# The fourth output product split into quarters, in blocks 3 to 8 of a linear-attention and feed-forward kernel

## The chip, the cores and the metric

The kernel runs on one core of a Trainium2 chip. The metric is the time of the whole kernel on the device in microseconds (us), as the median of several runs. The profile comes from one further execution, which has its own time.

## The reference

There are 8 batches of 576 tokens with 8 heads of 64 features, all in float32, so 4608 rows of 512 features. Cut to what matters:

```
kv  = einsum('bhsd,bhse->bhde', k, v)
att = einsum('bhsd,bhde->bhse', q, kv)
att = att / sqrt(mean(att * att, axis=-1) + 1e-06) * g_norm
x   = att, laid out as (4608, 512)
h   = x @ w_in                 # (4608, 512) @ (512, 2048)
g   = maximum(0.01 * h, h)     # leaky relu
out = g @ w_out                # (4608, 2048) @ (2048, 512)
```

The two products with `w_in` and `w_out` are nearly all of the work.

## The kernel before

**Blocks and chunks.** The rows are worked in 9 blocks of 512 tokens, i = 0 to 8. The 2048 hidden features are worked in 4 chunks of 512, c = 0 to 3. For a block and a chunk there is a hidden product (512 features of h for 512 tokens), a leaky relu, and an output product that adds its share to the block's 512x512 output. The text calls the output product of block i and chunk c pass n, with n = 4(i - 1) + c. Block 0 is done plainly. From block 1 on there are 32 passes, n = 0 to 31.

**Strassen's method.** Both products are cut into 2x2 parts and done with 7 products of parts instead of 8, in Winograd's form. Some factors are sums of parts. For the left side these are made by GpSimd in `sums_of` (L840), from g, into the tiles gs1 to gs4. For the right side they are made once from `w_out` and kept in device memory (`w2_dram`); SP loads them again for every pass, in `sides_w2` (L663), into the tiles `t12` and `t34`. `strassen` (L797) runs the products. In the output, products 1, 6, 7 and 4 go one after the other into one PSUM bank and add up there; products 2, 5 and 3 go into another. The two banks are called oa and oc and change roles from pass to pass. Each product is four matmuls of 128 rows by 256 columns. After each one, `done` (L990) adds the bank, or copies it where chunk 0 begins a fresh output, into one of the block's four output tiles, which are named 11, 12, 21 and 22 for their place in the 2x2 output.

**A second level.** From block 2 on the hidden product is done with two levels (`product_h_two`, L931): seven steps k = 1, 2, 6, 5, 7, 3, 4, each of seven matmuls of 128x128 in two of the banks ha, hb, hc, hd. The second bank of each step has three columns of 128 in use. The fourth column takes one quarter of the output's product 2 of an earlier pass, which is also done with a second level (`Second`, L906), so a hidden step is eight matmuls of 128x128. After the step ScalarE copies, or VectorE adds, the first three or four columns to the quarter sums `qa` and `qc` (L952, L954), and then VectorE adds the fourth column to the output tile. `inner_g` (L894) makes the sums of g's quarters that `Second` needs, on GpSimd.

**The order of the work.** It is written out by hand. A loop over the blocks, the chunks and seven slots t = 0 to 6 issues in each slot first one hidden step, then attention's next piece for a later block, then one step of the output product (`go_o`). The output product runs late: product 1 of pass n comes at slot 2 of the following chunk, product 5 at slot 3, product 6 at slot 4, nothing at slot 5, product 7 at slot 6, and products 3 and 4 at slots 0 and 1 of the chunk after that. At a chunk's end VectorE assembles g from the quarter sums with seven adds (L960 to L969), ScalarE applies the relu to the four parts of g, and GpSimd starts `sums_of`. `pin` keeps each engine's instructions in the order in which they are written; each engine works through its own instructions in that order. Inside a block, chunk 3's slots 20 to 22 also form the sums of the next block's x, on VectorE.

## Time and profile before

| what | value |
|---|---|
| median of 3 runs | 918.76 us (918.22 to 924.06) |
| the profiled execution | 917.78 us, span 916.1 us |
| TensorE busy (matmuls) | 909.3 us, 99% |
| VectorE busy | 631.6 us, 69% |
| ScalarE busy | 328.2 us, 36% |
| GpSimd busy | 370.2 us, 40% |
| DMA traffic | 200.05 MB |

In the profile PE is TensorE, DVE is VectorE, ACT is ScalarE, POOL is GpSimd, and SP is the queue that issues most DMAs. A group's line has the source line, the engine, the operation, `out<-in` by tile names, the shapes, the count, the busy time, the mean of one in ns, and the idle time of the engine just before, with what ended it. A line of the timeline has the start, the duration, the engine and the instructions merged; idle time ahead of it stands in brackets. A float32 matmul appears as two records, so a product of four matmuls is `x8`. The end of a matmul in the records is modelled; the distance between starts is safer. All engines' adds are issued by one helper (L637), so a group is told by its tiles. A line of the list of waits gives who waited, for whom, the total in us, the number of times and the longest.

### The profile page before, as it was taken

The page shows a single profiled execution, that of the slowest core. Times are in us where ns is not written, and L with a number is a line of the kernel's source. Part 1 is how long each engine was busy: PE and PEld are TensorE (multiplying, and loading weights), DVE is VectorE, ACT ScalarE, POOL GpSimd, SP SyncE. Part 2 cuts the span into 40 slices and gives each one's busy share as a digit, 9 for nine tenths or more (in the row PEclk, how much of TensorE's full clock was granted, in tenths as well). Part 3 has the DMA queues.
Part 4 walks back from the last instruction along what each step waited for, and adds up shares of the span by engine and source line. Part 5 has one row for each costly group of instructions (what it writes and reads, how often), then busy time and mean ns, then how long its engine had stood idle before and what let it go on. Part 6 is the DMA issues. An engine that isn't in the chain of part 4 may idle for free.

```text
span 916.1 us, 18037 instructions
## 1 busy us (share of the span) xinstructions
PE 909.3 (99%) x6980; PEld 776.3 (85%) x6980; DVE 631.6 (69%) x1168; ACT 328.2 (36%) x645; POOL 370.2 (40%) x438
## 2 busy tenths in 40 slices
PE   9999999999999999999999999999999999999998
PEld 5444448888998999899999999999999999999997
DVE  4876995587457876587756786678659755755565
ACT  5454533242135233533343324332343333223330
POOL 2000355967633473226421642264226422642222
DMA  8999926885599778776886789658765676667632
GB/s 269 236 245 249 248 85 191 280 285 167 166 360 289 228 209 268 233 230 214 255 247 230 219 249 272 222 178 212 242 183 176 187 222 198 185 185 223 197 109 92
DMA packets 90228, 200.05 MB, mean 218 GB/s; under 512 B 9888, under 2 KB 42272, under 8 KB 90144
## 3 DMA queue, kind: packets, MB, share of 16 engines
q1 hardware_dynamic: 79680, 187.04, 68.6%
q10 hardware_dynamic: 10016, 10.69, 3.4%
q8 instruction: 55, 0.90, 0.4%
q0 software_dynamic: 448, 1.18, 0.3%
q14 instruction: 29, 0.24, 0.1%
HBM read 172.39 MB, written 26.48 MB: 217 GB/s over the span
## 4 chain that ended last, share of the span: by engine, by line
PE 96%; DMA 2%; DVE 1%; issue 0%; ACT 0%; POOL 0%; SPq 0%; ACTq 0%; DVEq 0%; POOLq 0%
PE o_a L118 19%; PE o_c L118 18%; PE h_ha L118 11%; PE h_hb L118 11%; PE h_hc L118 8%; PE h_hd L118 8%; PE o_acc L118 6%; PE h_ps L118 6%; PE o_ps L118 3%; PE h_a L118 2%; PE h_b L118 1%; PE h_c L118 1%; PE h_d L118 1%; PE kv_ps L118 1%; DMA pairs<-in_v_dram 1%; DMA v_in<-in_v_dram 1%
## 5 line engine op out<-in xcount | busy, mean ns | idle before, releaser
L637 POOL TENSOR_TENSOR gs<-g 128x512 f32<-128x512 f32 x64 | 81.7, 1277 | 253.3 <-ACT g L833 253.3
L833 ACT ACTIVATE g<-g 128x512 f32<-128x512 f32 x124 | 78.2, 631 | 131.9 <-DVE g L637 131.9
L952 ACT COPY w_all<-h_ha 128x512 f32<-128x512 f32 x84 | 48.9, 582 | 173.5 <-PE h_ha L118 167.8
L118 PE MATMUL o_a<-pairs,gs 128*128 128x256 f32 x384 | 91.3, 381 | 0.0
L118 PE MATMUL o_c<-pairs,gs 128*128 128x256 f32 x376 | 89.2, 380 | 0.0
L637 DVE TENSOR_TENSOR o<-h_hb,o 128x128 f32<-128x128 f32 x104 | 29.8, 287 | 83.8 <-ACT pairs L952 83.7
L637 DVE TENSOR_TENSOR o<-o_c,o 128x512 f32<-128x512 f32 (+1 forms) x91 | 61.2, 672 | 23.9 <-PE o_c L118 23.6
L118 PEld LDWEIGHTS o_a<-pairs,gs 128*128 128x128 f32 x384 | 69.8, 190 | 9.2 <-POOL pairs L637 1.2
L118 PEld LDWEIGHTS o_c<-pairs,gs 128*128 128x128 f32 x376 | 68.3, 190 | 7.6
L637 DVE TENSOR_TENSOR o<-o_a,o 128x512 f32<-128x512 f32 x75 | 51.2, 683 | 28.2 <-PE o_a L118 28.1
L637 POOL TENSOR_TENSOR pairs<-w_all 128x512 f32<-128x512 f32 x8 | 11.1, 1384 | 120.6 <-ACT cut L245 102.3
L118 PE MATMUL h_ha<-stage,w_all 128*128 128x128 f32 x448 | 59.6, 276 | 0.0
L118 PEld LDWEIGHTS h_ha<-stage,w_all 128*128 128x128 f32 x448 | 56.6, 192 | 3.0 <-issue 0.7
L118 PE MATMUL h_ps<-xT,w_all 128*128 128x512 f32 (+1 forms) x136 | 58.0, 570 | 0.9 <-DVE w_all L258 0.9
L118 PE MATMUL o_acc<-w,g 128*128 128x512 f32 x128 | 57.8, 595 | 0.0
L637 DVE TENSOR_TENSOR g<-g,pairs 128x512 f32<-128x512 f32 x84 | 55.7, 689 | 1.9
L637 POOL TENSOR_TENSOR pairs<-g 128x128 f32<-128x128 f32 x52 | 23.9, 459 | 75.4 <-PE h_hb L118 46.7
L118 PEld LDWEIGHTS h_ps<-xT,w_all 128*128 128x128 f32 x136 | 25.5, 190 | 30.0 <-issue 26.6
L637 DVE TENSOR_TENSOR w_all<-h_hc,w_all 128x512 f32<-128x512 f32 x56 | 38.3, 684 | 15.9 <-PE h_hc L118 15.8
L118 PEld LDWEIGHTS o_acc<-w,g 128*128 128x128 f32 x128 | 24.0, 190 | 29.8 <-issue 29.4
L637 DVE TENSOR_TENSOR o<-h_hd,o 128x128 f32<-128x128 f32 x78 | 22.1, 283 | 37.8 <-ACT pairs L952 37.7
L118 PE MATMUL h_hb<-stage,w_all 128*128 128x128 f32 x336 | 46.7, 275 | 0.0
(228 smaller groups left out, 2264.6 us busy)
## 6 DMA issues: line engine op xcount, KB each, us to landing
w_all<-w SPq DMA_DIRECT2D x196, 448.0 KB, 4.2
pairs<-w SPq DMA_DIRECT2D x56, 512.0 KB, 4.3
out_dram<-o ACTq DMA_DIRECT2D x35, 256.0 KB, 4.6
v_in<-in_v_dram SPq DMA_DIRECT2D x29, 288.0 KB, 5.7
k_in<-in_k_dram SPq DMA_DIRECT2D x28, 288.0 KB, 5.1
q_in<-in_q_dram SPq DMA_DIRECT2D x56, 144.0 KB, 6.0
q_in<-in_q_dram SPq DMA_DIRECT2D x56, 140.0 KB, 5.8
w<-stage SPq DMA_DIRECT2D x12, 512.0 KB, 4.6
```

The costliest lines, as they stand in the source:

```text
L118: pin(nc.tensor.matmul(*args, **kw))
L637: ins = eng.tensor_tensor(out_, a, b_, op=ALU.subtract if minus else ALU.add)
L833: nc.scalar.activation(t, t if src is None else src, func=AF.Prelu, alpha=SLOPE)
L952: nc.scalar.copy(q[:, at], bank)
```

## The change

For the passes n = 8 to 29 (blocks 3 to 8) product 4 of the output is no longer done as four matmuls of 256 columns. It is done as seven products of 128x128 quarters, one matmul each, in a new class `Fourth`.

- The seven quarters go into a new tile in the bank that products 1, 6 and 7 of the pass have used, as soon as product 7 has been taken out of it. They use three of the bank's four columns: quarters 1, 6, 7 and 4 the first, where they add up, quarter 2 the second, quarters 5 and 3 the third.
- They come in four steps: 1, 2, 5 right after product 3; 6 and 3 in the slot that product 4 had; 7 just before product 1 of the next pass; 4 just after it. After each quarter VectorE adds its column to the output tile 21 (ScalarE copies it where the output is fresh: quarters 1, 5, 6 and 4 of chunk 0).
- Products 1, 6 and 7 used to reach output 21 through the bank, since product 4 was added on top of them. Now their sum goes, with product 7, to a tile of its own, `os["7"]`, which adds up over a block's chunks. At the block's last changed pass VectorE adds it to 22 and to 21.
- `inner_g` makes its four sums for two of g's parts at once (128x256 instead of 128x128).
- The quarters of the right side and their sums (7 x 128 columns) are made once, on GpSimd in passes 4 to 7 (`inner_w4`), and kept in device memory. The load of `t34` becomes three DMAs (256, 256 and 192 KB) and is issued after quarter 4 instead of after product 4.
- Output tiles come from a pool of 4 and one of 2 instead of one of 6 and are taken when first written. `ident` moves into a tile of the x sums.

The diff, cut to its core:

```diff
+    w4_dram = [dram.tile([P, 7, P], F32, name=f"w4_{c}") for c in range(NC)]
+    t12, t34 = pair(2, 2, U, N2), view(pairs, 28 * P, 2, U, N2)
+    f4 = t34[:, 1].rearrange("p u (v n) -> p (u v) n", v=2)
+    f4_more = view(stage, 21 * P, 3, P)
+
+    def four(n):
+        return 2 * NC <= n < NC * (NB - 1) - 2
...
         def sums(i):
             t = (t12, t34)[i]
+            if four(n) and i:
+                pin(nc.sync.dma_start(t[:, 0], w2_dram[c][i][:, 0]))
+                pin(nc.sync.dma_start(f4, w4_dram[c][:, :4, :]))
+                pin(nc.sync.dma_start(f4_more, w4_dram[c][:, 4:, :]))
+                return
...
+    def inner_w4():
+        y11, y12, y21, y22 = (f4[:, k, :] for k in range(4))
+        t1, t3, t2 = (f4_more[:, k, :] for k in range(3))
+        add(nc.gpsimd, t1, y12, y11, True)
+        add(nc.gpsimd, t3, y22, y12, True)
+        add(nc.gpsimd, t2, y22, t1, True)
+        add(nc.gpsimd, y12, y21, t2, True)
...
     def inner_g(c, half):
-        g = g_of(c)[3]
-        a11, a21, a12, a22 = (g[:, n, :] for n in range(4))
-        s1, s2, s3, s4 = (gi[:, n, :] for n in range(4))
+        g = view(g_all[c % 2], 0, 4, 4, P)
+        a11, a21, a12, a22 = (g[:, n, 2:, :] for n in range(4))
+        s1, s2, s3, s4 = (gi_two[:, :, n * P:n * P + P] for n in range(4))
...
+    class Fourth:
+        STEPS = (1, 2, 5), (6, 3), (7,), (4,)
+        COLUMN = {1: 0, 6: 0, 7: 0, 4: 0, 2: 1, 5: 2, 3: 2}
...
+        def step(self, at):
+            if at == 0:
+                self.bank = ps_m.tile([P, 4, P], F32, tag=self.tag, name=f"f_{self.tag}")
+            for k in self.STEPS[at]:
+                bank = self.bank[:, self.COLUMN[k], :]
+                matmul(bank, lhsT=self.left[k], rhs=self.right[k], start=(k == 1), stop=True,
+                       skip_group_check=True)
+                v, s = INTO[k]
+                to = self.o_of("21")[:, v, s * P:s * P + P]
+                if self.n % NC == 0 and k in (1, 5, 6, 4):
+                    nc.scalar.copy(to, bank)
+                else:
+                    add(nc.vector, to, bank, to)
+            if at == 3:
+                self.last()
...
         def done(i, bank):
             key, fresh = into[i]
+            if fourth and i == 7:
+                key, fresh = "7", True
+            o_of(key)
...
-            if c == NC - 1 and i in (2, 7, 3, 4):
+            if fourth and i == 7:
+                if c == NC - 1 or not four(n + 1):
+                    add(nc.vector, os["22"], os["22"], os["7"])
+                if c == NC - 1:
+                    finish("22", os["22"])
+            elif c == NC - 1 and i in (2, 7, 3, 4):
                 finish(key, os[key])
...
+        def last():
+            sums(1)
+            if c == NC - 1 or not four(n + 1):
+                add(nc.vector, os["21"], os["21"], os["7"])
+            if c == NC - 1:
+                finish("21", os["21"])
+
+        tags = (("oa", "oc"), ("oc", "oa"))[n % 2]
+        order = (1, 5, 6, None, 7, 3, None if fourth else 4) if second else ORDER
+        before = fourths.popleft() if fourths else None
+        if fourth:
+            now = Fourth(n, tags[0], o_of, last)
+            fourths.append(now)
+        steps = strassen(tags, lambda i, part, r: g_sides[i][:, 2 * r + part, :],
+                         lambda i, part, r: w_sides[i][:, r, :], done, order, pieces=pieces)
+        for j in range(7):
+            if before and j == 0:
+                before.step(2)
+            next(steps)
+            if before and j == 0:
+                before.step(3)
+            if fourth and j > 4:
+                now.step(j - 5)
+            yield
```

## The prediction

> **What bounds the kernel now.** I read the page first (busy time, then the chain that ended last), then the list of waits and the groups by form, and last the timeline around one place where the change sits.

> ```profile
> PE 909.3 (99%) x6980; PEld 776.3 (85%) x6980; DVE 631.6 (69%) x1168; ACT 328.2 (36%) x645; POOL 370.2 (40%) x438
> ...
> PE 96%; DMA 2%; DVE 1%; issue 0%; ACT 0%; POOL 0%; SPq 0%; ACTq 0%; DVEq 0%; POOLq 0%
> ```

> TensorE is the bound, and it hardly ever waits. A gain has to be TensorE time; but any wait newly laid on TensorE is added to the end at full price. So I ask of each new matmul what it waits for, and how late that is. The timeline of pass n = 15 (chunk 3 of a block) shows it, TensorE first, then VectorE, then ScalarE:

> ```profile
> 545.34 1.89 PE L118 MATMUL o_a<-w,gs 128*128 128x256 f32 x8
> 547.07 0.38 PE L118 MATMUL h_hc<-xT,w_all 128*128 128x128 f32 x2
> ...
> 548.85 1.89 PE L118 MATMUL o_c<-pairs,g 128*128 128x256 f32 x8
> 550.58 1.05 PE L118 MATMUL h_ha<-stage,w_all 128*128 128x128 f32 x8
> ```

> ```profile
> 543.99 0.68 DVE L637 TENSOR_TENSOR o<-o_c,o 128x512 f32<-128x512 f32 x1
> 544.59 1.48 DVE L637 TENSOR_TENSOR g<-g,w_all 128x512 f32<-128x512 f32 x2
> 546.10 2.02 DVE L637 TENSOR_TENSOR g<-g,pairs 128x512 f32<-128x512 f32 x3
> 549.19 0.29 DVE L637 TENSOR_TENSOR o<-h_hb,o 128x128 f32<-128x128 f32 x1 [1.06 <-ACT pairs L952]
> 549.40 0.68 DVE L637 TENSOR_TENSOR o<-o_a,o 128x512 f32<-128x512 f32 x1
> 549.99 0.68 DVE L637 TENSOR_TENSOR w_all<-h_hc,w_all 128x512 f32<-128x512 f32 x1
> 550.59 0.55 DVE L637 TENSOR_TENSOR pairs<-h_hd,pairs 128x384 f32<-128x384 f32 x1
> 551.06 0.28 DVE L637 TENSOR_TENSOR o<-h_hd,o 128x128 f32<-128x128 f32 x1
> ```

> ```profile
> 548.16 0.63 ACT L833 ACTIVATE g<-g 128x512 f32<-128x512 f32 x1 [0.42 <-DVE g L637]
> 548.70 0.46 ACT L952 COPY pairs<-h_hb 128x384 f32<-128x384 f32 x1
> ```

> At 545.34 TensorE starts product 3. It is through with it at 547.07 (four matmuls of 256 columns, 1.73 us), yet VectorE adds it out of its bank only from 549.40 to 550.08. The reason is a chain that every chunk boundary has: VectorE assembles g (seven adds), ScalarE applies the last relu, only then copies the hidden product's bank (548.70), only then VectorE may read that bank's fourth column (549.19), and product 3 stands behind that. Call D the time from the start of product 3's matmuls to the end of its add: 4.74 us here. Today nobody needs this add soon, so the delay is free. TensorE doesn't stop.

> D from the same two rows at all 22 places that change: chunk 0 (n = 8, 12, ... 28): 5.70, 5.28, 4.85, 4.74, 4.74, 4.73. Chunk 1: 7.27 five times (the block sums of x stand in VectorE's queue there), 4.73 for n = 29. Chunk 2: 5.33, 5.16, 5.27, 5.38, 4.73. Chunk 3: 4.74 five times.

> [...] the small adds from the fourth column of a hidden bank never start before ScalarE's copy of the other columns has ended, though both only read:

> ```profile
> DVE o L637 <- ACT pairs L952: 121.5, 91, 3.2
> ```

> [...] four passes of 512 columns take 3.78 us from 1.53 us on, and 1.88 us from 8.12 us on. Later it has no long gap, so what a gap of some 4 to 6 us costs there no run shows.

> ```profile
> 1.53 3.78 PE L118 MATMUL idle_ps<-g 128*128 128x512 f32 x4 [1.53 <-DVE group L294]
> ...
> 8.12 1.88 PE L118 MATMUL idle_ps<-g 128*128 128x512 f32 x4
> ```

> **The change part by part.** *Matmuls.* Removed per pass: four matmuls of 256 columns, 1.73 us. Added: seven of 128 columns. A hidden step is eight of these and takes 1.78 us (547.07 to 548.85), so 0.22 us each, 1.56 us. Gain 0.17 us, times 22: 3.8 us. That is all there is to win.

> *Where the quarters stand.* All seven go into one bank: quarters 1, 2, 5 straight after product 3 (step A), 6 and 3 after the next hidden step (B), 7 before the next pass's product 1 (C), 4 after it. Each is added out by VectorE (in chunk 0, where the output is fresh, four of the seven by ScalarE). [...] the second quarter's matmul carries a wait on VectorE's counter, at the number of the first quarter's add; the fifth, sixth and third likewise. And the first quarter's add stands in VectorE's queue behind product 3's add, which is late by D.

> *Prices of a turn.* An add of 128x128: 0.28 us, next one 0.21 us after it. From a matmul's last column to the start of its reading: 0.20 us (hidden step ends 552.37, ScalarE's copy starts 552.57). From an add to the waiting matmul: the trace of before has hardly such a case; ScalarE's copy to VectorE is 0.03 us (549.16 to 549.19), a weight load takes 0.19 us. Bounds 0 to 0.3 us; I take 0.1.

> *Step A.* Unhindered it would end 1.73 + 0.67 = 2.40 us after product 3's start. Now: D + 0.21 + 0.1 until quarter 2 may start, 0.22 for it, 0.20 + 0.28 + 0.1 until quarter 5 may start, 0.22 for it: D + 1.33. Lost: D - 1.07. In chunk 0 ScalarE takes quarter 1 beside product 3's add, and quarter 5 waits for D + 0.31: lost D - 1.87. Sums: chunk 1: 5 x 6.20 + 3.66 = 34.7. Chunk 2: 20.5. Chunk 3: 5 x 3.67 = 18.3. Chunk 0: 18.8. Together 92.3 us.

> *Joint sum.* At chunk 3 VectorE adds os["7"] to the 22 output inside the chain that makes D: 0.60 us (the pitch of a 128x512 add), five times: 3.0 us. The other such add, to 21, stands after quarter 4 and nobody waits. Product 7's own add costs what it did.

> *Step B.* Quarter 6 waits for quarter 5's add, done by then. Quarter 3 waits for quarter 6's add, and that stands behind the three adds of the hidden step (the last ends about 0.95 us after the step, by the 0.60, 0.47 and 0.28 of the rows above): lost 1.0 us. In chunk 1 another sum of x stands between (1.07 us): 2.1. In three passes of chunk 2 a transpose of q_in (1.25 us): 2.2. In chunk 0 ScalarE is free: 0.55. Together 10.0 + 3.6 + 10.5 + 3.3 = 27.4 us.

> *Step C.* Quarter 4 waits for quarter 7's add; between lies product 1, 1.73 us. That covers a turn (0.6 us), but behind a transpose, or attention's sums, VectorE comes late, read off where product 1's add starts today: chunk 1 0.7 us four times and 2 us at n = 21, chunks 2 and 3 0.5 us in three passes each, chunk 0 0.43 us in four: 9.5 us. Quarter 4's own add is covered by the hidden step before product 5.

> *The clock.* Between quarters 1 and 2 TensorE idles D - 1.64: 5.6 us in chunk 1, 3.1 to 3.7 in chunks 2 and 3. [...] I take 2 us at the five of chunk 1: 10 us.

> *What stays covered.* GpSimd's four sums of g double to 256 columns (459 to 744 ns, 1.15 us a pass); before its next work it idles 8 us at the boundary. The load for the next pass's products 7 and 4 becomes three DMAs, 704 instead of 512 KB, and moves behind quarter 4 in SP's queue, so the reads of hidden weights that follow it wait too; these run five slots ahead (17 us against 4.2 us to landing), and product 7 comes four slots (14 us) later. If that cover went, one landing, 4.3 us a pass. Bytes: 22 x 192 KB on 200 MB. The quarter sums of the weights are made once, on GpSimd, 4 x 0.46 us in each of four passes, and stored; the passes before n = 8 have room. Fewer o buffers: each is asked for again a block later, at least three slots after its store (4.6 us).

> *Sum.* 92.3 + 3.0 + 27.4 + 9.5 = 132.2; less 3.8: +128.4; clock +10: +138. The profiled execution took 917.8 (span 916.1 and 1.7 around it): 1056. The median of the runs is 1.0 above it: 1057.

> **Rivals.** *Clock falls at nearly every gap.* Fifteen gaps of 3.1 us and more[...], in place of the 10: 917.8 + 128.4 + 51 + 1 = 1098. For it: the start of the trace[...]. *Waits by column alone.* If a quarter held back only what writes its own column, step A is free, and quarters 6 and 3 lose D - 3.67 (32.5 us over all), C and the joint sum stay: 917.8 + 32.5 + 12.5 - 3.8 + 1 = 960. For it: the data need no more; against it: the 91 waits above. *Not slower.* VectorE is 31% idle and might have every quarter out before TensorE asks: 915 on the median, the bare gain. This decides itself on D: with bank waits the loss ends at D = 1.07, by column at 3.67; the smallest D in the trace is 4.73, and the two chains that make it (g and the relus) aren't touched. *Shorter chain:* TensorE's pauses let VectorE catch up before the boundary and D shrinks; but D counts from the boundary itself, where VectorE has been idle 1.59 us at n = 15. If D shrank by 1 us at every place: 1035.

> **How the numbers follow.** Forecast 0.80, clock rival 0.08, column rival 0.07, not slower 0.03, shorter chain 0.02. The forecast's own range: the release at 0 or 0.3 instead of 0.1 in three turns of 22 passes gives -7 and +13, the clock -10 and +40, the reading of C and B some 15 either way: 1010 to 1100. That holds the clock rival too in part, and leaves about 2 in 10 out. A change within 1% is about what a measurement of this kernel cannot tell from none: faster 0.01, within 0.03, slower 0.96.

> **What would show it.** Right: gaps of TensorE of 3 to 6 us inside the run of f_oa or f_oc matmuls, released by VectorE's adds into o (ScalarE's copies in chunk 0), longest in chunk 1; TensorE's share of the span near 86%; hidden steps outside the quarters at their old pitch. Half-speed matmuls after the long gaps would show the clock part, and none would take 10 us off. Wrong: quarters 1, 2 and 5 back to back at 0.22 us, or D below 4 us in the new trace.

## The result, and the profile after

The changed kernel takes 1088.74 us (median of 4 runs, 1086.73 to 1093.2) against 918.49 us beside it (4 runs, 918.19 to 924.06): a ratio of 1.184, 95% interval 1.179 to 1.190. The forecast was 1057 us with a range of 1010 to 1100. The profiled execution took 1087.84 us, with a span of 1086.0 us.

The page of the changed kernel: the row of TensorE's busy time, the row of its granted clock (tenths of full speed, 40 slices of the span), and the chain that ended last.

```profile
PE 966.6 (89%) x7112; PEld 819.2 (75%) x7112; DVE 664.1 (61%) x1288; ACT 333.4 (31%) x669; POOL 401.6 (37%) x454
...
PEclk9999999999999998899988899989989999998989
...
PE 66%; DVE 15%; DMA 9%; ACT 4%; POOL 3%; issue 3%; SPq 0%; ACTq 0%; DVEq 0%
```

TensorE falls from 99% of the span to 89%, and the chain that was TensorE's at 96% now runs over VectorE, DMAs, ScalarE and GpSimd for a third of its length. Two things stand in these rows. The span holds 119 us in which TensorE does nothing (before: 7). And TensorE is busy 57 us longer, with matmuls that should have been 4 us shorter: the clock row shows eights from its 16th slice on (407 us), shortly after the first changed pass (383 us).

The list of waits (who waited, for whom: total us, times, longest):

```profile
PE f_oc L118 <- DVE o L638: 61.0, 26, 5.3
...
PE f_oa L118 <- DVE o L638: 22.3, 13, 3.4
...
PE f_oa L118 <- ACT o L978: 7.9, 10, 2.2
```

The three rows with f_oc and f_oa did not exist before. They are the quarters' matmuls, waiting for the add or the copy of the quarter ahead of them: 91 us in these rows alone. Some 16 us more of such waits stand in rows that name GpSimd, a DMA or nothing as the one waited for; the list infers this name, and the experiment without reads below shows that none of these waits is left when the quarters' adds and copies are gone.

The timeline of pass n = 15, the place that the prediction showed, first TensorE:

```profile
608.60 1.89 PE L118 MATMUL o_a<-w,gs 128*128 128x256 f32 x8
610.33 0.39 PE L118 MATMUL f_oc<-pairs,g 128*128 128x128 f32 x2
614.52 0.79 PE L118 MATMUL f_oc<-pairs,g 128*128 128x128 f32 x2 [3.81 <-DVE o L638]
615.75 0.76 PE L118 MATMUL f_oc<-stage,pairs 128*128 128x128 f32 x2 [0.43 <-POOL gs L638]
616.30 0.64 PE L118 MATMUL h_hc<-xT,w_all 128*128 128x128 f32 x2
616.73 0.63 PE L118 MATMUL h_hc<-w_all 128*128 128x128 f32 x2
```

then ScalarE's copy of the hidden bank, and VectorE:

```profile
612.89 0.46 ACT L1005 COPY pairs<-h_hb 128x384 f32<-128x384 f32 x1
```

```profile
608.25 0.69 DVE L638 TENSOR_TENSOR o<-o,o 128x512 f32<-128x512 f32 x1
608.85 1.41 DVE L638 TENSOR_TENSOR g<-g,w_all 128x512 f32<-128x512 f32 x2
610.30 2.02 DVE L638 TENSOR_TENSOR g<-g,pairs 128x512 f32<-128x512 f32 x3
613.38 0.29 DVE L638 TENSOR_TENSOR o<-h_hb,o 128x128 f32<-128x128 f32 x1 [1.06 <-ACT pairs L1005]
613.59 0.68 DVE L638 TENSOR_TENSOR o<-o_a,o 128x512 f32<-128x512 f32 x1
614.18 0.28 DVE L638 TENSOR_TENSOR o<-f_oc,o 128x128 f32<-128x128 f32 x1
615.35 0.29 DVE L638 TENSOR_TENSOR o<-f_oc,o 128x128 f32<-128x128 f32 x1 [0.89 <-PE f_oc L118]
```

Read the two engines against each other. Quarter 1 is multiplied at 610.33. VectorE can't take it out before 614.18: the joint add (608.25), the five adds of g shown, the wait of 1.06 us for ScalarE's copy and product 3's add (613.59) stand ahead. The add ends at 614.46, and quarter 2 starts at 614.52. From product 3's start to the end of its add it is 5.67 us here, where it was 4.74: the joint add accounts for 0.6. After the gap TensorE's rows change: a pair of records that starts 0.22 us after the one before it at full speed starts 0.43 us after it (616.30, 616.73). That is half clock: the clock records grant 0.5 from 613.91 to 620.74. In front of quarter 5 the view names GpSimd, but the add of quarter 2 ends at 615.64 and quarter 5 starts 0.1 us later, as it does in all 22 passes; so this is the turn again.

**Where the 170 us are.** I take one period per pass, from the start of its product 3 to the start of the next pass's. The 22 changed passes are 162.5 us longer in all. 2.0 us more come just ahead of them, nearly all between passes 6 and 7, and 0.6 us behind them. The other 4.9 us are at the start, ahead of pass 0: there TensorE waits 2.2 us for a load of v, then runs 3.4 us at half clock, and later waits 0.8 us for another. That part moves between -0.8 and +8.7 us from kernel to kernel in the experiments, though they all share the changed kernel's start, so it is not put down to the change.

### The profile page after: what moved, and what is told of

Its sections match the earlier page's. It is cut to its first block, busy times and chain, and to the rows that moved or that the text cites. A ratio compares the mean times of both kernels' runs of the same rounds, so it can differ in the third digit from the quotient of the medians.

```text
span 1086.0 us, 18588 instructions
## 1 busy us (share of the span) xinstructions
PE 966.6 (89%) x7112; PEld 819.2 (75%) x7112; DVE 664.1 (61%) x1288; ACT 333.4 (31%) x669; POOL 401.6 (37%) x454
## 4 chain that ended last, share of the span: by engine, by line
PE 66%; DVE 15%; DMA 9%; ACT 4%; POOL 3%; issue 3%; SPq 0%; ACTq 0%; DVEq 0%
PE o_a L118 10%; PE o_c L118 10%; DVE g L638 9%; PE h_hc L118 8%; PE h_ha L118 8%; PE h_hd L118 8%; PE h_hb L118 7%; DVE o L638 3%; POOL gs L638 3%; PE o_acc L118 3%; DMA stage<-in_moe_w_in_dram 2%; PE o_ps L118 2%; PE f_oc L118 2%; DMA v_in<-in_v_dram 2%; DMA pairs<-in_moe_w_in_dram 2%
## 5 line engine op out<-in xcount | busy, mean ns | idle before, releaser
L638 POOL TENSOR_TENSOR pairs<-g 128x256 f32<-128x256 f32 x52 | 38.3, 736 | 170.1 <-PE h_hd L118 127.4
L118 PE MATMUL o_a<-pairs,gs 128*128 128x256 f32 x384 | 91.4, 381 | 0.0
L118 PE MATMUL o_c<-pairs,gs 128*128 128x256 f32 x376 | 89.3, 380 | 1.5 <-DVE g L638 1.5
L118 PEld LDWEIGHTS o_a<-pairs,gs 128*128 128x128 f32 x384 | 69.8, 190 | 9.4 <-POOL pairs L638 1.2
L118 PEld LDWEIGHTS o_c<-pairs,gs 128*128 128x128 f32 x376 | 68.3, 190 | 9.3 <-DVE g L638 1.7
L638 DVE TENSOR_TENSOR o<-o_c,o 128x512 f32<-128x512 f32 (+1 forms) x80 | 53.7, 672 | 25.5 <-PE o_c L118 25.1
L638 DVE TENSOR_TENSOR o<-o_a,o 128x512 f32<-128x512 f32 x64 | 43.8, 684 | 29.5 <-PE o_a L118 29.3
L118 PE MATMUL h_ha<-stage,w_all 128*128 128x128 f32 x448 | 61.1, 280 | 0.0
L118 PE MATMUL f_oc<-pairs,g 128*128 128x128 f32 x66 | 16.9, 344 | 49.1 <-DVE o L638 49.0
L118 PE MATMUL h_ps<-xT,w_all 128*128 128x512 f32 (+1 forms) x136 | 58.0, 570 | 0.9 <-DVE w_all L259 0.9
L118 PE MATMUL o_acc<-w,g 128*128 128x512 f32 x128 | 58.8, 604 | 0.0
L118 PEld LDWEIGHTS h_ha<-stage,w_all 128*128 128x128 f32 x448 | 56.5, 196 | 1.9 <-issue 0.7
L118 PEld LDWEIGHTS f_oc<-pairs,g 128*128 128x128 f32 x66 | 12.7, 218 | 54.5 <-DVE o L638 53.8
L118 PE MATMUL h_hd<-xT,w_all 128*128 128x128 f32 x224 | 51.9, 320 | 0.0
L118 PE MATMUL h_hc<-xT,w_all 128*128 128x128 f32 x224 | 50.9, 315 | 0.0
```

Of the source, the lines that this page charges most:

```text
L118: pin(nc.tensor.matmul(*args, **kw))
L638: ins = eng.tensor_tensor(out_, a, b_, op=ALU.subtract if minus else ALU.add)
```

## The experiments

The table gives for each what the 22 passes lost against the kernel before (by the same periods), and how it divides. Waits are read in front of each quarter: the idle time, plus 0.16 us, since a matmul normally starts so much before the modelled end of the one ahead (610.33 against 608.60 + 1.89 above). A, B and C are the prediction's steps. The matmuls' bare gain, 3.2 us, is taken from the run without reads below. The clock is the remainder: loss + 3.2 - waits. (Read from the clock record instead, for the changed kernel: its passes hold 105.8 us at half clock, in which TensorE is busy for 85.1 us; half of that, 42.6 us, is what half clock added.)

| kernel | ratio to before | loss of the passes | A | B | C | clock |
|---|---|---|---|---|---|---|
| after | 1.184 | 162.5 | 90.2 | 25.2 | 5.1 | 45.2 |
| matmuls first | 1.072 | 61.0 | 0 | 43.4 | 5.4 | 15.4 |
| spread, one at a time | 1.159 | 137.4 | 81.1 | 18.2 | 1.1 | 40.2 |
| spread, matmuls first | 1.017 | 11.0 | 0 | 2.1 | 1.6 | 0 |

In the last row most of the loss is in other products, told there.

### Matmuls first, then the adds

```
-            for k in self.STEPS[at]:
-                bank = ...; matmul(bank, ...)
-                add(nc.vector, to, bank, to)
+            for k in self.STEPS[at]:
+                matmul(self.bank[:, self.COLUMN[k], :], ...)
+            for k in self.STEPS[at]:
+                add(nc.vector, to, self.bank[:, self.COLUMN[k], :], to)
```

> The changed kernel with one edit: within each step the matmuls of its quarters are issued first and their adds after them, so no quarter of a step waits for the add of the quarter before. Theory (turns of one bank, each behind product 3's late add): step A loses nothing, step B waits once for A's last add (D - 3.45, 45 us over the 22 passes with the joint sum), step C stays at 9.5 us, and few gaps are left that reach the clock: 970 to 990 us. Rival (VectorE simply has too many small adds, seven for one): the same adds are made in the same number, so 1080 to 1090 us.

Measured: 988.91 us, ratio 1.072 (1.066 to 1.077). TensorE in the same pass n = 15:

```profile
580.97 1.89 PE L118 MATMUL o_a<-w,gs 128*128 128x256 f32 x8
582.70 0.61 PE L118 MATMUL f_oc<-pairs,g 128*128 128x128 f32 x4
583.14 0.39 PE L118 MATMUL f_oc<-stage,pairs 128*128 128x128 f32 x2
583.37 0.39 PE L118 MATMUL h_hc<-xT,w_all 128*128 128x128 f32 x2
...
587.24 0.46 PE L118 MATMUL f_oc<-stage,pairs 128*128 128x128 f32 x2 [1.92 <-DVE o L638]
```

Quarters 1, 2 and 5 now stand back to back and the hidden step follows at full speed: step A costs nothing. Nothing about the bank, the columns, the number of adds or the delay of product 3's add was touched (it is 5.4 us in this pass); only the turns between the quarters went. So it is not the number of VectorE's adds that cost these 100 us. The delay comes back in part one step later: quarter 6 writes the bank that the adds of A have not left yet, and waits 1.92 us. So 100 us of the 170 are the order inside a step, and with matmuls first the placement decides the rest.

### The gap filled with needless matmuls

Behind quarter 1, TensorE does 7, 20, 11 or 11 more matmuls of 128x128 (chunks 0 to 3) into the bank's unused fourth column. They compute nothing that is used. The wait stays where it was, but TensorE isn't idle in it.

```
+                for _ in range((7, 20, 11, 11)[self.n % NC] if k == 1 else 0):
+                    matmul(self.bank[:, 3, :], lhsT=self.left[1], rhs=self.right[1], ...)
```

> The changed kernel, and between quarter 1 and quarter 2 a few needless matmuls of 128 columns into the bank's unused fourth column (7, 20, 11, 11 for chunk 0, 1, 2, 3; 1.6 to 4.5 us), so that TensorE works through most of the wait. Nothing else changes. Theory (about 50 us of the loss is TensorE at half clock after these gaps, the waits themselves are untouched): mean granted clock from 0.949 to 0.99 or more, 1035 to 1050 us. Rival (the clock is low for another reason, or the half clock lies under waits anyway): within 10 us of 1088 us.

Measured: 1057.98 us, ratio 1.148 (1.143 to 1.154), with a mean granted clock of 0.991 in the profiled execution where after had 0.949. The delay of product 3's add is the same to 0.02 us in every pass. The passes lose 134.3 us, 28 us less, with 272 needless matmuls of 0.22 us in place of pauses. A kernel that does more work is 31 us faster, because its clock stays up (0.991 against 0.949). The clock is thus a cost of its own, beside the wait. Not all of the 45 us goes. The clock records still hold 13.7 us at half clock in these passes, which is worth some 6.5 us. The filling overruns the wait at six places: quarter 2 comes 0.5 to 1.5 us later than in the changed kernel in five passes of chunk 0, and 1.3 us later at n = 29. And behind matmuls at full clock the next turns wait a little longer (quarter 5 mostly 0.70 us instead of 0.59). By the same reading that leaves about 3 us which no term holds. The time is 8 us above the expected range for these reasons and for the stall at passes 6 to 7 (5.3 us), which the next two runs explain.

### Without the quarters' reads

The quarters are multiplied but never added to the output, which is set to zero on GpSimd; so their adds and copies are left out, and with them every wait on these.

```
-                add(nc.vector, to, bank, to)        # or ScalarE's copy
+                if self.n % NC == 0 and k == 1:
+                    pin(nc.gpsimd.memset(self.o_of("21"), 0.0))
```

> The changed kernel without the reads of the seven quarters out of their bank (output 21 is left without product 4; a memset starts it). The matmuls, GpSimd's wider sums, the three loads and the joint sum all stay. Theory (all of the loss is waits for these reads and what follows from them): 914 to 922 us, TensorE at 99% from pass 8 on. Rival (the wider sums on GpSimd, or the larger loads moved behind quarter 4 in SP's queue, carry part of it): 930 us or more, with TensorE waiting for POOL or DMA.

Measured: 922.27 us, ratio 1.001 (0.998 to 1.003). The 22 passes take 3.2 us less than before; a pass without other waits takes 22.70 us instead of 22.87, the 0.17 us of the prediction. So the wider sums on GpSimd, the three loads and the joint sums cost TensorE nothing there. But the period from pass 6 to 7 is 30.12 us instead of 22.87. The chain of waits of that stretch, in order of time (start, us, what):

```profile
339.92 3.42 POOL stage L638 x6
...
344.16 0.47 POOL pairs L638
...
344.65 2.06 DMA w<-pairs
...
346.72 6.83 DMA pairs<-w
...
353.68 3.75 PE o_c L118 x8
```

This is the preparation of the quarter sums, which the prediction gave "room". GpSimd makes them in the half of `t34` that product 4 has left, behind its sums of x; then SP stores them (344.65), and only then loads `t34` for the next pass (346.72). The load lands at 353.55, and product 7 of n = 7 has been waiting for it for 4.30 us. It then runs at half clock: 3.75 us for what takes 1.89.

### The late load undone

The same kernel without reads, with the half of `t34` that product 7 reads loaded right at product 4 in passes 4 to 7. Only the half in which the sums are made still waits.

```
             elif i == 4 and NC <= n < 2 * NC:
+                sums(1, 0)                  # first half at once
                 inner_w4()
...
-                    [2, lambda: sums(1)]))
+                    [2, lambda: sums(1, 1)]))
```

> The kernel without the quarters' reads once more, with one more edit: in passes 4 to 7 the half of the next pass's pair that product 7 reads is loaded at product 4, as in the kernel before, and only the half in which the quarter sums are made waits two slots. Theory (the 7.3 us lost at passes 6 to 7 came from this load's late issue alone): that stall goes, the passes keep their gain of 0.17 us each, and the time is 914 to 917 us, ratio to before 0.994 to 0.998. Rival (the load is late for another reason, such as SP's queue being held, or the half clock comes from elsewhere): it stays at 921 to 923 us.

Measured: 916.77 us, ratio 0.998 (0.997 to 1.000). SP's queue and TensorE at the place:

```profile
333.33 0.42 SPq L682 DMA_DIRECT2D pairs<-w  x1
```

```profile
348.82 1.89 PE L118 MATMUL o_c<-pairs,gs 128*128 128x256 f32 x8
```

The load is issued at 333.33, 13 us earlier, and product 7 starts with no wait. The period from 6 to 7 is 22.87 us again and the passes keep their 3.2. That settles the stall. It also gives the ceiling: with every wait on the quarters' reads gone, and their work with them, the whole change is worth 0.2% (0.0 to 0.3% by the interval).

### Spread out, and matmuls first

The kernel without reads was one half of the answer: what is the loss when the reads stay, but TensorE comes to them later? Here step A stands one slot later (after the hidden step that follows product 3's slot), B behind product 1 of the next pass, 7 and 4 one slot later each. The next pass's product 5 moves behind the empty slot, so that it doesn't ask for the quarters' bank early. The part of `t34` that product 7 reads is loaded right after product 7. Inside a step the matmuls come first.

```
-        order = (1, 5, 6, None, 7, 3, None if fourth else 4) if second else ORDER
+        order = ORDER if not second else (1, 6, None, 5, 7, 3, None) if fourth else \
+            (1, 5, 6, None, 7, 3, 4)
...
+            for at in ((1,), (2,), (3,))[j] if before and second and j < 3 else \
+                    (1, 2, 3) if before and not second and j == 0 else ():
+                before.step(at)
+            if fourth and j == 6:
+                now.step(0)
```

> The changed kernel with the quarters spread out: matmuls of a step ahead of its adds; quarters 1, 2, 5 a slot later (where product 4 was), 6 and 3 behind the next pass's product 1, 7 a slot after that, 4 another slot later; products go 1, 6, nothing, 5, 7, 3 so that product 5 finds the bank free; the load for product 7 is issued after product 7, apart from the quarters' load. All work is kept. Theory: every turn now has at least 1.7 us of other TensorE work under it and D is no longer in the way, so the bare gain of 3.8 us less what precedes pass 8 shows: 914 to 925 us. Rival (VectorE's number of adds, or the loads): above 940 us.

Measured: 936.59 us, ratio 1.017 (1.013 to 1.020), so nine tenths of the loss are gone. What TensorE still waits for, from the list of waits:

```profile
PE o_c L118 <- DMA pairs<-w: 4.2, 1, 4.2
PE o_a L118 <- DVE o L638: 3.3, 5, 1.1
PE f_oc L118 <- DVE o L638: 3.0, 4, 1.0
```

The first row is the late load (6.8 us with the half clock behind it). The others lie in chunks 1 and 2 only. The six passes of chunk 1 are 1.0 to 2.3 us longer each than they would be without waits. In all six one hidden step waits for the add out of its bank (0.2 to 0.3 us idle). At n = 21 and 25 the block sums of x stand in VectorE's queue ahead of A's adds, and quarter 6, once also product 1, waits for it. At n = 29, behind which the last steps follow each other at once, quarters 7 and 4 wait. The smaller waits of n = 9, 13 and 17, in front of the next products, aren't followed up here. In chunk 2 product 5 waits for quarter 4's add behind attention's work (0.7 to 1.4 us longer in four passes). Chunks 0 and 3 lose nothing.

### Spread out, but one at a time

The last kernel with the quarters' adds back between the matmuls of a step.

> The steps stand as far apart as in the kernel that spread them (the first step a slot after product 3, the second behind the next pass's first slot, quarters 7 and 4 a slot each later), but within a step each quarter's add again stands ahead of the next quarter's matmul. Theory (the turns within a step are the main cost, because quarter 2's matmul waits for quarter 1's add, which stands behind whatever VectorE has in its queue): spreading alone helps little; step A still loses about the delay of one add in every pass, some 85 us, step B some 15, half clock some 30 of it: 1030 to 1055 us. Rival (the place of the steps was the main cost, and what the matmuls-first order saved it saved by moving step B's reads apart): 940 to 970 us.

Measured: 1064.31 us, ratio 1.159 (1.157 to 1.162), somewhat above the range that the theory gave; the late load (6.3 us) was not in it, and the clock took 40 us instead of 30.

```profile
PE f_oc L118 <- DVE o L638: 53.8, 25, 5.8
...
PE f_oa L118 <- DVE o L638: 19.2, 11, 3.3
```

The rival, that the places were the main cost, is out. Spreading alone saves 24 us of the 170; taking the turns out alone saves 100; both together 152. The wait is the turn's: moved a slot later, quarter 2 still waits 5.8 us in chunk 1 and 2.2 to 3.3 us in chunks 2 and 3 (0.9 us at n = 29, 0.35 us in chunk 0), because the add of quarter 1 stands behind what VectorE's queue holds at that place too.

### Only where it costs nothing

The spread order, matmuls first and the early load, with the second level only in chunks 0 and 3 of blocks 3 to 8 (11 passes instead of 22).

```
-        return 2 * NC <= n < NC * (NB - 1) - 2
+        return 2 * NC <= n < NC * (NB - 1) - 2 and n % NC in (0, NC - 1)
```

> The spread placement with matmuls first, the early load, and the second level only in chunks 0 and 3 of a block (11 passes instead of 22), where the spread kernel's passes lost nothing. Theory (what was left of the loss were VectorE's queue in chunks 1 and 2 and the late load): 915 to 919 us, ratio to before 0.996 to 1.001, the 11 passes gaining 0.17 us each, less up to 2 us for the joint sums. Rival (the spread order itself costs, also in chunk 1 that now has another order of products and a split load): 922 to 930 us.

Measured: 917.15 us, ratio 1.000 (0.998 to 1.002). The page:

```profile
PE 907.2 (99%) x7046; PEld 776.7 (85%) x7046; DVE 644.5 (71%) x1222; ACT 333.0 (36%) x669; POOL 410.2 (45%) x454
...
PE 96%; DVE 2%; DMA 1%; ACT 0%; POOL 0%; issue 0%; ACTq 0%; DVEq 0%; POOLq 0%
```

TensorE is the bound again, at a mean granted clock of 1.000. The passes in question take 1.6 us less than before (0.16 us each in ten of them, nothing at n = 15), and the list of waits has no quarter's matmul any more. The median can't tell this from no change.

## Why the prediction was right, and what in it was off

- **The mechanism.** Each quarter's matmul waits for the add ahead of it, and the first of these adds is late by product 3's add: shown by the timeline, and by taking out the turns alone.
- **The gain, 3.8 us.** 3.2 measured, in the runs without reads; 0.17 us in a pass without other waits.
- **Step A with the joint sum, 92.3 + 3.0 us.** 90.2 measured. Chunk 1: 34.7 against 34.7 forecast, in part by luck: the working left out that the joint sum stands at the last changed pass, n = 29, too (D is 5.39 there, 4.74 before), and the other five have a D shorter by 0.06 to 0.08 us. Chunk 3: 21.7 against 18.3 and the joint sum's 3.0; D is 5.39 in four of its five passes, 0.65 above the 4.74 of before, 5.67 in one. Chunk 2: 19.7 against 20.5. Chunk 0: 14.1 against 18.8; there D did get shorter, by 0.67 us in each pass (5.70 became 5.03, 4.73 became 4.07). That isn't the rival's reason, a VectorE that catches up while TensorE pauses. The prediction said "Product 7's own add costs what it did", and in chunk 0 it doesn't: `os["7"]` is fresh there, so ScalarE copies product 7 out, and an add of 0.68 us has left VectorE's queue ahead of product 3's. At n = 20, before and after:

```profile
664.33 0.68 DVE L637 TENSOR_TENSOR o<-o_a,o 128x512 f32<-128x512 f32 x1
```

```profile
766.34 0.58 ACT L1064 COPY o<-o_a 128x512 f32<-128x512 f32 x1 [1.21 <-PE o_a L118]
```

- **A turn's release, taken as 0.1 us within 0 to 0.3.** In the changed kernel it is 0.05 us for quarter 2, 0.10 us for quarter 5 and 0.15 us for quarter 3.
- **Step B, 27.4 us.** 25.2 measured, with n = 29 (1.1 us), which the sum had left out.
- **Step C, 9.5 us.** 5.1 measured. In chunk 1 it is 0.7 us instead of 4.8: the delays of product 1's add read off the kernel before didn't carry over. Probably VectorE had caught up while TensorE was late; no run shows that apart.
- **The clock, 10 us.** This is the term that was furthest off: about 45 us measured. The prediction charged 2 us at the five gaps of 5.3 us in chunk 1 and nothing for the gaps of chunks 2 and 3. But half clock came with each of the 17 gaps in front of quarter 2 that last 2.22 to 5.34 us, and twice more (n = 24 and 28) with a gap of 1.25 us and the 0.51 us in front of quarter 5. So there were 19 places, not five; at each the cost was 2.4 us on average, not far from the 2 us assumed. Eight of the stretches last 3.41 us, ten 6.83 us and one 10.24 us. The clock rival (1098 us) had the size nearly right, 51 us for 15 places. Both prices of a place, the 2 us and the rival's, were assumptions: no trace had shown one. The rival summed too high mostly because its waits were the forecast's, 132.2 us against 120.5 measured (90.2 + 25.2 + 5.1).
- **"The passes before n = 8 have room."** Wrong, by 2.0 us in the changed kernel, where the load landed 4.3 us after its issue, and by 7.3 us in the run without reads, where it took 6.8 us and half clock followed. The step counted GpSimd's time and left out that the load for the next pass's product 7 was queued behind the store of these sums. The early load took the stall away.
- **The other covers** (the wider sums, three loads behind quarter 4, fewer output buffers) held: no wait for them is left in the run with the early load.

The waits were over by 12 us and the clock under by 35; with the late load and the start that is the difference of 32 us to the median forecast. The measured time lies inside the range because its upper side held 40 us for the clock, an assumption too, and most of these were used. The 5 us at the start have nothing to do with the argument.

The rival of waits by column alone fell with the first timeline: quarter 2 writes a column that nobody reads, and waits (3.81 us at n = 15). A kernel with such waits wasn't tried. Whether the chip would need the add between two columns of one bank can't be said from these runs; with the matmuls of a step ahead of its adds, quarters 1, 2 and 5 go into three columns 0.22 us apart, and no add stands between them.

## What to carry to other kernels

Before splitting a product, ask for each piece which engine must act between it and the next, and how late that engine is at that very place: a delay that nobody feels (product 3's add, 4.7 to 7.3 us from its matmuls' start in the kernel before) was paid here, 90.2 us over the 22 passes, once TensorE took turns with it. If pieces share a bank, issue all their matmuls first and read them afterwards (that alone took 100 of the 170 us away), and put the next step that writes this bank behind the reader's longest stretch (with it, the ratio was 1.017 instead of 1.072). Price a pause of the bounding engine twice, for its length and for what its clock does afterwards (here 2.4 us more on average at each of 19 places); and follow each load that a preparation displaces to the instruction that waits for it, since in the run without reads the order in SP's queue cost 7.3 us, which a count of GpSimd's free time had not shown.

## What the runs showed of the hardware

The mean granted clock of the kernel before is 1.000. The clock records of the changed kernel grant 0.5 in 19 stretches of the changed passes, 105.8 us in all. The table sets TensorE's idle time in front of quarters 2 and 5 beside the stretch of half clock that began during one of these pauses or within 1.3 us after it:

| chunk | pass n | idle before quarter 2, us | idle before quarter 5, us | half clock, us |
|---|---|---|---|---|
| 0 | 8 | 2.22 | 0.51 | 3.41 |
| 0 | 12 | 0.42 | 1.88 | none |
| 0 | 16 | 1.36 | 0.51 | none |
| 0 | 20 | 1.25 | 0.51 | none |
| 0 | 24, 28 | 1.25 | 0.51 | 3.41 |
| 1 | 9, 13, 17, 21, 25 | 5.33 to 5.34 | 0.43 | 6.83 |
| 1 | 29 | 3.53 | 0.43 | 6.83 |
| 2 | 10, 14, 18 | 3.12, 3.23, 3.33 | 0.43 | 6.83, 10.24, 6.83 |
| 2 | 22, 26 | 3.44, 2.80 | 0.43 | 3.41 |
| 3 | 11, 19, 23 | 3.53 | 0.43 | 3.41 |
| 3 | 15, 27 | 3.81, 3.53 | 0.43 | 6.83 |

The length of the pauses alone doesn't settle it: 1.25 and 0.51 us were followed by half clock at n = 24 and 28 and not at n = 20, and 3.53 us came with a stretch of 3.41 us three times and of 6.83 us twice. What else decides is not shown. No stretch began with the pauses in front of quarter 3, which last up to 1.80 us (n = 18).
